# Attention weights split out of the PSUM bank that holds the exponentials, in a fused attention and gated-MLP kernel

## The chip, the core and the metric

The kernel runs on one core of a Trainium2 chip. The metric is the device time of one execution in microseconds, the median over the runs shown. Five engines work side by side, each through its own queue in order: TensorE (PE; its weight loads are PEld), VectorE (DVE), ScalarE (ACT), GpSimd (POOL) and SyncE (SP, which here only issues DMAs). Matmuls write to PSUM, which has 8 banks of 512 float32 values per partition; everything else is in SBUF. POOL does not work on PSUM in this kernel: whatever it reads lies in SBUF.

## What is computed

Eight batches of 448 tokens. Attention with 12 heads of 64, with normalised q and k, and then an MLP that is gated across tokens:

```python
# attention, per batch and head; q, k, v: (8, 12, 448, 64)
q_n, k_n = rmsnorm(q, g_q), rmsnorm(k, g_k)
scores = (1 / 8) * q_n @ k_n.T
attn = exp(scores - max(scores, axis=-1))
attn = attn / (sum(attn, axis=-1) + 1e-9)
x = attn @ v                                   # heads joined: (8, 448, 768)
# MLP
h = gelu_tanh(x @ w_in)                        # 768 -> 1024
u, v = h[..., :512], h[..., 512:]
v_n = (v - mean(v)) / sqrt(var(v) + 1e-6) * g_ln
v_s = einsum('ts,bsd->btd', w_sg, v_n) + b_sg[None, :, None]
out = x + (u * v_s) @ w_out                    # 512 -> 768
```

## The kernel before

Matmuls run on 16-bit operands. To keep float32 accuracy most operands are split into a high part (float16 of the value) and a low part (float16 of what the high part leaves), and the products that matter are summed in PSUM.

**Attention.** Heads are done in pairs, 48 pairs in all, 6 to a batch. A pair has 896 rows of scores, cut into 7 tiles of 128 rows by 448 columns; tile 3 holds the tails of both heads. In `scores(i)` a tile goes through these steps:

- L411: two matmuls on PE (four for tile 3) write the scores into a PSUM bank `s`; there are `NS` = 4 such banks.
- L414: DVE takes the negated row maximum `nm`.
- L416: ACT takes the exponential, writes it to an SBUF tile `a` (`NA` = 4 buffers) and the row sums to a small SBUF tile `sums`. After this the bank `s` is free.
- L420 and L422: once per group of tiles (`RG`: tiles 0-1, 2-3, 4-6) DVE makes the scaled reciprocals `rc` of the row sums.
- L430 or L432: the high part `a * rc` as float16, by POOL for the tiles in `PT` (0, 3, 6; in the first batch `PT0`, 0, 2, 4, 6) and by ACT for the others.
- L433: the low part `a * rc - high` on DVE, after the high part.
- L436: SP issues a DMA that transposes the two parts of two tiles (one for the last) into `at`, which `pv` multiplies with v (L453, L455) one pair later.

POOL also does most of the splitting of q and k: L344, L345 and L348, for 47 pairs (the first is split on DVE). ACT also issues the loads of q and k (L269).

**MLP.** `moe(b)` runs one batch behind the attention, in steps that are woven into it. Its matmuls use `NM` = 3 PSUM banks: `mv_` (x times the v half of `w_in`, four tiles of tokens), `mu_` (the u half, four tiles of features), `ms_` (the mix across tokens), `mo_` (the output). Gelus run in clusters, since each cluster loads the gelu table and then the exp table. Tiles that must wait for their cluster stay in their bank, or are copied to SBUF first: `mv_` tile 3 (L523) and `mu_` tiles 0 and 1 (L580). For the first and the last batch (`early`) the `mv_` matmuls start while that batch's last heads are still to come: three token tiles advance together, block by block, and the short tile 3 follows.

**Order.** The code yields pieces of scores, pv, weights and MLP in fixed proportions, and a list scheduler then sets the order on each engine from priorities and buffers. So a change of the buffers or of the engine of one step moves the work around it too.

Of the kernel before, what the change touches and what calls it, by code (L numbers as in the profile page):

```python
# [8 lines left out]
F32 = mybir.dt.float32  # L9
# [14 lines left out]
# places in the order of the work that the MLP and its gelus are moved by  # L24
MOFF, MOFF0, GP = 200, 100, 350
# steps of the weights and of the MLP per pair of heads (first, second, middle, last batch)
WR, M0, M1, MR, ML = 3, 8, 7, 11, 11
# pairs of heads at which the first MLP begins and by which the weights are done
I0, WD = 5, 6
# tiles of the scores that share a reciprocal; that are transposed together; whose high part GpSimd  # L30
# makes (in the first batch)
RG = ((0, 2), (2, 4), (4, 7))
TG = (2, 2, 2, 1)
PT, PT0 = (0, 3, 6), (0, 2, 4, 6)
# buffers
NS, NV, NM = 4, 1, 3
NQK, NVR, GV, RAWB = 2, 2, 3, 3
NA, NAH, NAT, NQT, NVH, HLB = 4, 4, 2, 2, 2, 2
# [6 lines left out]
def kernel(  # L45
# [64 lines left out]
    def newton(y, x, t):  # L110
        """y, a guess of x ** -0.5 within 3.5%, made better by a step of third and one of second order."""
# [8 lines left out]
    def pow2_scale(name, part, pool):  # L120
        """part [rows, n] holds sums of squares. Gives the power of two that takes
        every element of the tensor below 2^14 * 1.04, and its inverse."""
# [16 lines left out]
    W = {}  # L139

    def decode(dst, raw, tmp):
        """float64 words (low, high) to float32; magnitudes below float32's normal range give 0."""
# [10 lines left out]
    def weights():  # L153
        nonlocal mlp
        ctx_w = ExitStack()
        # w_in's parts take the place of its float32 values, one K block after the other
# [46 lines left out]
        # w_sg with its rows and columns in the order of the tokens on chip, and the  # L203
        # last 64 columns twice, so that both halves of the partitions get them
# [51 lines left out]
    # A head's tokens on chip: 128 c + p is token 3 p + c for c < 3 (blocks m0, m1, m2), 384 + p the  # L256
    # tail t. A pair of heads A, B is 7 columns of 128 rows: A's m0, m1, m2, then the tails of A and B
    # in one, then B's m0, m1, m2; so A's keys are in the order (m0, m1, m2, t), B's in (t, m0, m1, m2).
# [32 lines left out]
    def load_v(i):  # L291
        """A head's v in 7 columns: m0, m1, m2, (t, m0a), (m0b, m1a), (m1b, m2a), (m2b, t), with a and b
        the halves of a block: what meets the blocks of A's transposed weights and, from (t, m0a) on, of B's."""
# [17 lines left out]
    def v8(x):  # L311
        """Of a pair's columns A's 0..3 and B's 3..6."""
        return bass.AP(tensor=x.tensor, offset=x.offset, ap=[list(x.ap[0]), [10 * D, 2], [1, 4 * D]])
# [43 lines left out]
    def vsquares(i):  # L357
        """The sums of squares of the GV pairs of heads from i on."""
# [30 lines left out]
    def parts_of(t):  # L389
        """Tile t of a pair's 896 rows of scores: (rows of the tile, head)."""  # L390
        if t == CM:
            return [(0, HP, 0), (HP, P, 1)]
        return [(0, P, t // CK)]

    def scores(i):
# [4 lines left out]
        r["at"] = at  # L400
        for t0, t1 in RG:
            sums = sml.tile([P, 4], F32, name="sums")
            rc = sml.tile([P, 4], F32, name="rc")
            tl = []
            for t in range(t0, t1):
                ps = ps_s.tile([P, S], F32, name="s")
# [8 lines left out]
                a = att.tile([P, S], F32, name="a", bufs=NA)  # L415
                A.activation(out=a, in_=ps, func=AF.Exp, bias=nm, accum_out=sums[:, t - t0:t - t0 + 1])  # L416
                tl.append((t, a))
# [5 lines left out]
            for t, a in tl:  # L423
# [5 lines left out]
                if t in (PT if i >= NP else PT0):  # L429
# [55 lines left out]
    def moe(b, early=False):  # L485
# [20 lines left out]
        for st, (t, g) in enumerate(steps):  # L506
# [18 lines left out]
            if early and t == CM - 1 and g == NP - 1:  # L525
                cluster([gelu_v(i) for i in range(CM)], done)
# [269 lines left out]
```

## Time and profile before

| | |
|---|---|
| median of 3 runs (lowest to highest) | 1049.12 us (1044.31 to 1051.55) |
| span of the profiled execution | 1047.2 us, 17092 instructions |
| busy: PE / PEld / DVE / ACT / POOL | 809.6 / 447.3 / 899.9 / 705.4 / 504.6 us |
| the same as a share of the span | 77% / 43% / 86% / 67% / 48% |
| high parts made by ACT / by POOL | 186 / 150 |
| DMA | 177.74 MB, mean 170 GB/s |

Busy time is what an engine's instructions took; waiting and issuing DMAs are not in it. A row of groups reads: line, engine, operation, output tile <- input tiles, shapes, x count | busy us, mean ns of one | idle time of the engine just before them and what ended it. A bank or buffer that is late shows up as idle time of the instruction that needs it, ended by the one that freed it. Matmul records overlap each other, so a high busy share of PE does not by itself make it the limit.

### The profile page before, as it was taken

What the parts mean: (1) busy time and instruction counts of PE and PEld (TensorE: products, weight loads), DVE (VectorE), ACT (ScalarE), POOL (GpSimd) and SP (SyncE); (2) the same over time, 40 slices, a digit from 0 to 9 for tenths busy, and PEclk for the clock granted to TensorE, in tenths of its full rate; (3) what the DMA queues carried; (4) which work ended last, traced back from release to release, by engine and by line L of the source; (5) the groups of instructions that cost most, each with busy time, mean ns of one, the idle gap of its engine ahead of it and who ended that gap; (6) DMA issues with size and microseconds to landing.
All of it is one profiled execution on the core that took longest, in us unless ns stands there. A gap on an engine that the chain in (4) does not pass through costs nothing. (4 is left out here: it accounts for less than half of the span.)

```text
span 1047.2 us, 17092 instructions
## 1 busy us (share of the span) xinstructions
PE 809.6 (77%) x5652; PEld 447.3 (43%) x5652; DVE 899.9 (86%) x1959; ACT 705.4 (67%) x1418; POOL 504.6 (48%) x435
## 2 busy tenths in 40 slices
PE   0333556757689798888979899887979799799998
PEld 0111222424454346444644357343634365346546
DVE  4999979999789997999979998999889988999430
ACT  2565787676677777677767767587667686877441
POOL 1777745637536463443545372545455443535021
PEclk9666688888899899899999899999989999999999
DMA  5969589685989979996797879994989779838501
GB/s 144 254 174 244 125 179 215 160 185 108 207 180 206 194 156 206 173 217 152 162 213 181 167 149 196 202 211 106 207 190 195 148 166 201 180 89 174 110 1 61
DMA packets 528217, 177.74 MB, mean 170 GB/s; under 512 B 472257, under 2 KB 521985, under 8 KB 528129
## 3 DMA queue, kind: packets, MB, share of 16 engines
q1 hardware_dynamic: 484928, 144.07, 66.6%
q10 hardware_dynamic: 43200, 32.59, 11.3%
q8 instruction: 44, 0.72, 0.3%
q14 instruction: 45, 0.36, 0.1%
HBM read 54.58 MB, written 11.01 MB: 63 GB/s over the span
## 5 line engine op out<-in xcount | busy, mean ns | idle before, releaser
L433 DVE SCALAR_TENSOR_TENSOR ahl<-a,rc,ahl 128x448 f16<-128x448 f32 x336 | 289.6, 886 | 32.1 <-POOL ahl L430 22.0
L416 ACT ACTIVATE a<-s,nm 128x448 f32<-128x448 f32 x336 | 211.0, 630 | 124.7 <-DVE ahl L433 78.0
L411 PE MATMUL s<-qt 128*128 128x448 f16 (+1 forms) x768 | 192.2, 388 | 120.8 <-ACT a L416 63.5
L430 POOL TENSOR_SCALAR ahl<-a,rc 128x448 f16<-128x448 f32 x150 | 117.3, 786 | 230.0 <-DVE rc L422 99.9
L414 DVE TENSOR_REDUCE nm<-s 128x1 f32<-128x448 f32 x336 | 200.2, 610 | 18.5 <-PE s L411 18.0
L432 ACT ACTIVATE ahl<-a,rc 128x448 f16<-128x448 f32 x186 | 118.1, 662 | 61.5 <-DVE rc L422 34.2
L411 PEld LDWEIGHTS <-qt 128*128 128x128 f16 (+1 forms) x768 | 57.2, 105 | 209.2 <-issue 127.8
L345 POOL TENSOR_TENSOR qk<-qk,ny 128x896 f32<-128x896 f32 x47 | 83.2, 1792 | 70.6 <-DVE ny L118 34.4
L348 POOL TENSOR_TENSOR hl<-qk,hl 128x896 f16<-128x896 f32 x47 | 95.7, 2037 | 34.4 <-ACT hl L347 26.3
L453 PE MATMUL pv<-at,vl 128*64 128x384 f16 x384 | 68.2, 368 | 56.7 <-DMA at<-ahl 44.8
L344 POOL TENSOR_TENSOR qk<-qk,gg 128x448 f32<-128x448 f32 x47 | 58.9, 1255 | 77.0 <-ACT sqk L324 76.8
L453 PE MATMUL pv<-at,vh 128*64 128x384 f16 x672 | 91.0, 357 | 0.0
L575 PEld LDWEIGHTS <-wi 128*128 128x128 f16 x576 | 57.4, 102 | 61.8 <-issue 15.9
L455 PE MATMUL pv<-at,vh 128*64 128x64 f16 x672 | 78.7, 202 | 0.0
L611 POOL TENSOR_TENSOR gt<-gt,u 128x448 f32<-128x448 f32 x32 | 39.0, 1221 | 79.0 <-DVE gt L610 59.2
L453 PEld LDWEIGHTS <-vl 128*64 128x64 f16 x384 | 30.7, 118 | 90.0 <-DMA at<-ahl 37.0
L416 ACT ACTIVATION_READ_ACCUMULATOR a<-s,nm 128x1 f32 x336 | 65.9, 196 | 0.0
L325 DVE TENSOR_REDUCE ss<-sqk 128x14 f32<-128x896 f32 x48 | 51.5, 1073 | 15.5 <-ACT sqk L324 15.2
L347 ACT ACTIVATE hl<-qk 128x896 f16<-128x896 f32 x48 | 45.3, 945 | 25.6 <-DMA qk<-in_k_dram 11.4
L324 ACT ACTIVATE sqk<-qk 128x896 f32<-128x896 f32 x48 | 45.3, 944 | 21.7 <-DVE ss L325 11.2
L453 PEld LDWEIGHTS <-vh 128*64 128x64 f16 x672 | 50.2, 120 | 18.6 <-issue 0.8
L420 DVE TENSOR_SCALAR rc<-sums 128x2 f32<-128x2 f32 x144 | 52.1, 364 | 7.1 <-ACT a L416 6.5
(995 smaller groups left out, 2096.0 us busy)
## 6 DMA issues: line engine op xcount, KB each, us to landing
qk<-in_k_dram ACTq DMA_DIRECT2D x48, 192.0 KB, 3.6
vr<-in_v_dram SPq DMA_DIRECT2D x16, 576.0 KB, 4.9
vr<-in_v_dram SPq DMA_DIRECT2D x32, 288.0 KB, 5.9
out_dram<-ot ACTq DMA_DIRECT2D x24, 384.0 KB, 3.8
qk<-in_q_dram ACTq DMA_DIRECT2D x46, 192.0 KB, 3.6
raw<-in_moe_w_in_dram SPq DMA_DIRECT2D x12, 512.0 KB, 4.9
vr<-in_v_dram SPq DMA_DIRECT2D x32, 96.0 KB, 4.9
at<-ahl SPq DMA_TRANSPOSE x192, 3.8
```

The costliest lines, as they stand in the source:

```text
L344: E.tensor_tensor(out=qk[:, C7:], in0=qk[:, C7:], in1=gg.unsqueeze(1).broadcast_to([P, C7, D]), op=ALU.mult)
L345: E.tensor_tensor(out=qk, in0=qk, in1=r["rs"].unsqueeze(2).broadcast_to([P, SSW, D]), op=ALU.mult)
L348: E.tensor_tensor(out=hl[:, 0:SSW, 1], in0=qk, in1=hl[:, 0:SSW, 0], op=ALU.subtract)
L411: mm(out=ps[p0:p1], lhsT=qt[:, t * P + p0:t * P + p1], rhs=qt[:, k0:k0 + S], start=(n == 0), stop=(n == 1))
L414: V.tensor_reduce(out=nm, in_=ps, axis=AX.X, op=ALU.max, negate=True)
L416: A.activation(out=a, in_=ps, func=AF.Exp, bias=nm, accum_out=sums[:, t - t0:t - t0 + 1])
L430: G.tensor_scalar(out=hl[:, 0], in0=a, scalar1=sc, scalar2=1.0, op0=ALU.mult, op1=ALU.mult)
L432: A.activation(out=hl[:, 0], in_=a, func=AF.Copy, scale=sc)
L433: V.scalar_tensor_tensor(out=hl[:, 1], in0=a, scalar=sc, in1=hl[:, 0], op0=ALU.mult, op1=ALU.subtract)
L453: mm(out=o[:, 0:SM].rearrange("p (c n) -> p c n", c=CM), lhsT=w, rhs=at[:, h * CK:h * CK + CM, blk], start=(n == 0), stop=(n == n_s - 1), ...
L455: mm(out=o[:, SM:S], lhsT=w, rhs=at[:, CM, blk, h * HP:(h + 1) * HP], start=False, stop=(n == n_s - 1), skip_group_check=True)
L575: done = mm(out=ps[:, 0:S], lhsT=ww[:, g, f * P:(f + 1) * P], rhs=xx, start=(n == 0), stop=(n == 17))
```

## The change

It does four things.

1. The exponential (L419 now) overwrites the scores in their own bank: `a` and its four buffers are gone. The row sums of a group go to columns 448 to 451 of the bank of the group's first tile.
2. The high part is made from that bank by ACT for every tile; POOL has none left. DVE makes the low part (L433 as before) from the bank too. The bank is free only after that.
3. There are 5 score banks in place of 4, and 2 MLP banks in place of 3 (one bank for pv as before, 8 in all).
4. The MLP copies `mv_` tiles 3 and 0 to SBUF before the gelus (before: 3 alone; `VC`), and in the first and last batch only two token tiles advance block by block; the others follow one by one.

```diff
-PT, PT0 = (0, 3, 6), (0, 2, 4, 6)
+VC, UC = (3, 0), (0, 1)
-NS, NV, NM = 4, 1, 3
+NS, NV, NM = 5, 1, 2
-NA, NAH, NAT, NQT, NVH, HLB = 4, 4, 2, 2, 2, 2
+NAH, NAT, NQT, NVH, HLB = 4, 2, 2, 2, 2
...
         for t0, t1 in RG:
-            sums = sml.tile([P, 4], F32, name="sums")
...
-                ps = ps_s.tile([P, S], F32, name="s")
+                bank = ps_s.tile([P, 512], F32, name="s")
+                ps = bank[:, 0:S]
+                if t == t0:
+                    sums = bank[:, S:S + 4]
...
-                a = att.tile([P, S], F32, name="a", bufs=NA)
-                A.activation(out=a, in_=ps, func=AF.Exp, bias=nm, accum_out=sums[:, t - t0:t - t0 + 1])
-                tl.append((t, a))
+                A.activation(out=ps, in_=ps, func=AF.Exp, bias=nm, accum_out=sums[:, t - t0:t - t0 + 1])
+                tl.append((t, ps))
...
-                if t in (PT if i >= NP else PT0):
-                    G.tensor_scalar(out=hl[:, 0], in0=a, scalar1=sc, scalar2=1.0, op0=ALU.mult, op1=ALU.mult)
-                else:
-                    A.activation(out=hl[:, 0], in_=a, func=AF.Copy, scale=sc)
-                V.scalar_tensor_tensor(out=hl[:, 1], in0=a, scalar=sc, in1=hl[:, 0],
+                A.activation(out=hl[:, 0], in_=ps, func=AF.Copy, scale=sc)
+                V.scalar_tensor_tensor(out=hl[:, 1], in0=ps, scalar=sc, in1=hl[:, 0],
                                        op0=ALU.mult, op1=ALU.subtract)
...
-        steps = [(t, g) for t in (CM, *range(CM)) for g in range(NP)]
+        order = (CM, *range(CM))
+        steps = [(t, g) for t in order for g in range(NP)]
         if early:
-            steps.sort(key=lambda x: (x[1], x[0]))
-            steps = [x for x in steps if x[0] < CM] + [x for x in steps if x[0] == CM]
+            steps = ([(t, g) for g in range(NP) for t in range(2)]
+                     + [(t, g) for t in order for g in range(NP) if t == CM or t > 1])
...
-            if t == CM and g == NP - 1 and not early:
-                A.activation(out=vg[:, tiles[t][1]], in_=ps[:, 0:FH], func=AF.Copy)
+            if t in VC and g == NP - 1 and not early:
+                A.activation(out=vg[:, tiles[t][1]], in_=ps[:, 0:DH if t < CM else FH], func=AF.Copy)
...
-            if early and t == CM - 1 and g == NP - 1:
-                cluster([gelu_v(i) for i in range(CM)], done)
+            if early and t == 1 and g == NP - 1:
+                cluster([gelu_v(i) for i in range(2)], done)
```

The scheduler moves a good deal around this. The next listings show three places; the names in brackets are what an instruction waits for (an engine, or a DMA queue, with the semaphore's number).

On PE, score matmuls of a pair in the middle of the kernel. Before, when a bank comes free:

```order
L411 LDWEIGHTS qt
L411 MATMUL s<-qt 128x448 [waits Activation_49]
L411 LDWEIGHTS qt
L411 MATMUL s<-qt 128x448
L411 LDWEIGHTS qt
L411 MATMUL s<-qt 128x448 [waits Activation_49]
L411 LDWEIGHTS qt
L411 MATMUL s<-qt 128x448
L411 LDWEIGHTS qt
L411 MATMUL s<-qt 64x448 [waits Activation_49]
L411 LDWEIGHTS qt
L411 MATMUL s<-qt 64x448
```

And now, in a batch's pair behind the `mu_` matmuls:

```order
L415 LDWEIGHTS qt [waits DMAHW5_49]
L415 MATMUL s<-qt 128x448 [waits DVE_49]
L415 LDWEIGHTS qt
L415 MATMUL s<-qt 128x448
L415 LDWEIGHTS qt [waits DVE_49]
L415 MATMUL s<-qt 128x448 [waits PE_49]
L415 LDWEIGHTS qt
L415 MATMUL s<-qt 128x448
L415 LDWEIGHTS qt
L415 MATMUL s<-qt 128x448 [waits DVE_49]
L415 LDWEIGHTS qt
L415 MATMUL s<-qt 64x448 [waits DVE_49]
```

The bank was released by ACT (the exponential); it is now released by DVE (the low part), and tiles come in longer rows, up to the five banks.

On ACT, exponentials (`s,nm`) and high parts (`rc`) of a middle pair. Before:

```order
L432 ACTIVATE ahl<-a,rc 128x448 [waits DVE_49,Activation_49]
L432 ACTIVATE ahl<-a,rc 128x448 [waits Activation_49]
L324 ACTIVATE sqk<-qk 128x896 [waits DMAHW6_49,DMAHW5_49,DMAHW7_49,DMAHW4_49,DMAHW0_49]
L416 ACTIVATE a,sums<-s,nm 128x448 [waits DVE_49] x2
L416 ACTIVATE a,sums<-s,nm 128x448 [waits DVE_49,PE_49]
L580 ACTIVATE u<-mu__6488 128x448 [waits PE_49]
```

And now:

```order
L419 ACTIVATE s<-s,nm 128x448 [waits Activation_49]
L419 ACTIVATE s<-s,nm 128x448 [waits DVE_49]
L419 ACTIVATE s<-s,nm 128x448 [waits PE_49,Activation_49]
L269 DMA qk<-in_k_dram 128x2x192 [waits DMAHW1_49]
L613 ACTIVATE gh<-gt 128x448 [waits Pool_49]
L432 ACTIVATE ahl<-s,rc 128x448 [waits DVE_49,Activation_49]
L432 ACTIVATE ahl<-s,rc 128x448
L432 ACTIVATE ahl<-s,rc 128x448 [waits DVE_49,Activation_49]
L432 ACTIVATE ahl<-s,rc 128x448
```

High parts of two or more tiles now stand in a row on ACT. Many exponentials wait for ACT itself, since the row sums of one tile go to the bank of another.

On DVE, low parts of a middle pair. Before:

```order
L386 SCALAR_TENSOR_TENSOR vl<-vr,v_s,vh 128x512 [waits DMAHW6_49,Activation_49]
L433 SCALAR_TENSOR_TENSOR ahl<-a,rc,ahl 128x448 [waits DMAHW3_49,Pool_49]
L433 SCALAR_TENSOR_TENSOR ahl<-a,rc,ahl 128x448 [waits DMAHW2_49,Activation_49]
L113 TENSOR_TENSOR nt<-nt,ny 128x28 [waits DVE_49]
L113 TENSOR_TENSOR lt<-lt,ly 128x4 [waits DVE_49]
L433 SCALAR_TENSOR_TENSOR ahl<-a,rc,ahl 128x448 [waits Activation_49]
L414 TENSOR_REDUCE nm<-s 128x1 [waits PE_49]
```

And now:

```order
L423 TENSOR_SCALAR rc<-s 128x3 [waits Activation_49]
L425 RECIPROCAL rc<-rc 128x3 [waits DVE_49]
L423 TENSOR_SCALAR rc<-s 128x2 [waits Activation_49]
L425 RECIPROCAL rc<-rc 128x2 [waits DVE_49]
L433 SCALAR_TENSOR_TENSOR ahl<-s,rc,ahl 128x448 [waits DMAHW1_49,Activation_49]
L433 SCALAR_TENSOR_TENSOR ahl<-s,rc,ahl 128x448 [waits Activation_49]
L433 SCALAR_TENSOR_TENSOR ahl<-s,rc,ahl 128x448 [waits DMAHW5_49,Activation_49]
L418 TENSOR_REDUCE nm<-s 128x1 [waits PE_49] x2
```

A low part waited for POOL or ACT; all now wait for ACT. The transposes that SP issues stay at 192.

More of the change, by code (lines that the diff above doesn't have):

```diff
@@ L422, in scores @@
             V.reciprocal(out=rc[:, 0:n], in_=rc[:, 0:n])
-            for t, a in tl:
+            for t, ps in tl:
                 if t in starts:
@@ L521, in moe @@
                                   rhs=ww[:, g, DH + e * FH:DH + (e + 1) * FH], start=first, stop=final)
-            if t == CM and g == NP - 1 and not early:
-                A.activation(out=vg[:, tiles[t][1]], in_=ps[:, 0:FH], func=AF.Copy)
+            if t in VC and g == NP - 1 and not early:
+                A.activation(out=vg[:, tiles[t][1]], in_=ps[:, 0:DH if t < CM else FH], func=AF.Copy)
                 psv[t] = vg[:, tiles[t][1]]
-            if early and t == CM - 1 and g == NP - 1:
-                cluster([gelu_v(i) for i in range(CM)], done)
+            if early and t == 1 and g == NP - 1:
+                cluster([gelu_v(i) for i in range(2)], done)
             if st % 2 == 1:
                 yield
-        cluster([gelu_v(t) for t in ((CM,) if early else (CM, *range(CM)))], done)
+        cluster([gelu_v(t) for t in order if not early or t == CM or t > 1], done)
         for t in range(CK):
@@ L578, in moe @@
                         yield
-            if f < 2:
+            if f in UC:
                 A.activation(out=u[f], in_=ps[:, 0:S], func=AF.Copy)
```

## The prediction

> **What bounds the kernel now.** I read the busy time by stage first (the table of windows), then the costliest groups of the long middle stage, then the spread of single durations, and last what each engine waited for. The stages are the first 300 us (weights and the first batch), 300 to 950 us, and the tail, where only the last MLP is left. The columns are the stretch, its length, and busy us (with the count of instructions) of PE, PEld, DVE, ACT and POOL, then the clock, DMA share and GB/s.
>
> ```profile
> core 0: us, PE busy (x) PEld busy (x) DVE busy (x) ACT busy (x) POOL busy (x), PEclk, DMA share, GB/s
> 0.00:300.00 300.00, 157.04 (x960) 78.36 (x962) 266.24 (x553) 191.33 (x384) 169.91 (x139) 0.78 0.79 182
> 300.00:950.00 650.00, 564.09 (x4079) 312.47 (x4077) 595.65 (x1320) 469.38 (x948) 315.44 (x272) 0.95 0.84 178
> 950.00:1047.20 97.20, 88.48 (x623) 56.42 (x619) 37.98 (x88) 44.72 (x88) 19.28 (x25) 0.99 0.34 79
> ```
>
> In the middle DVE is busy 595.65 of 650 us (91.6%), ACT 72%. PE shows 87%, but its records overlap and DVE hardly ever waits for it: the row of the row maximum (L414) below has 5.3 us of idle time ended by PE in 650. So the middle is bound by DVE, and the tail by PE (88.48 of 97.20). The groups of the middle stage that the change touches:
>
> ```profile
> L433 DVE SCALAR_TENSOR_TENSOR ahl<-a,rc,ahl 128x448 f16<-128x448 f32 x237 | 210.7, 914 | 26.4 <-POOL ahl L430 18.0 <-ACT ahl L432 8.4
> L416 ACT ACTIVATE a<-s,nm 128x448 f32<-128x448 f32 x237 | 148.8, 630 | 84.3 <-DVE ahl L433 47.5 <-DVE nm L414 23.7 <-DVE rc L420 3.6
> L414 DVE TENSOR_REDUCE nm<-s 128x1 f32<-128x448 f32 x237 | 140.5, 610 | 5.5 <-PE s L411 5.3
> L432 ACT ACTIVATE ahl<-a,rc 128x448 f16<-128x448 f32 x136 | 85.9, 662 | 38.2 <-DVE rc L422 18.0 <-issue 8.2 <-DVE nt L116 2.6
> L430 POOL TENSOR_SCALAR ahl<-a,rc 128x448 f16<-128x448 f32 x101 | 74.1, 738 | 157.2 <-DVE rc L422 61.6 <-DVE rc L420 15.4 <-DMA at<-ahl 12.5
> L420 DVE TENSOR_SCALAR rc<-sums 128x2 f32<-128x2 f32 x68 | 21.3, 317 | 1.3 <-ACT a L416 1.1
> L420 DVE TENSOR_SCALAR rc<-sums 128x3 f32<-128x3 f32 x34 | 13.4, 393 | 5.4 <-ACT a L416 5.2
> ```
>
> The low part (L433) is DVE's largest item, 914 ns in the mean. Its median is another number. The next rows give min/median/max of single instructions, and the timeline (start, us) one of the long ones beside what POOL does then:
>
> ```profile
> L433 DVE SCALAR_TENSOR_TENSOR ahl<-a,rc,ahl x336: 658/676/2397, 40.9 to 977.9; 128x448 f16<-128x448 f32 x168
> L420 DVE TENSOR_SCALAR rc<-sums x144: 128/159/1698, 34.3 to 975.5; 128x2 f32<-128x2 f32 x96, 128x3 f32<-128x3 f32 x48
> L414 DVE TENSOR_REDUCE nm<-s x336: 584/610/626, 28.8 to 973.5; 128x1 f32<-128x448 f32 x168
> L462 DVE SCALAR_TENSOR_TENSOR xl<-pv,xh x48: 585/611/625, 75.8 to 987.8; 128x448 f16<-128x448 f32 x48
> L610 DVE SCALAR_TENSOR_TENSOR gt<-ms__5332,gw,bb x1: 685/685/685, 495.8 to 495.8; 128x448 f32<-128x448 f32 x1
> L610 DVE SCALAR_TENSOR_TENSOR gt<-ms__6887,gw,bb x1: 655/655/655, 613.4 to 613.4; 128x448 f32<-128x448 f32 x1
> 649.38 2.40 DVE L433 SCALAR_TENSOR_TENSOR ahl<-a,rc,ahl 128x448 f16<-128x448 f32 x1
> 649.40 1.89 POOL L348 TENSOR_TENSOR hl<-qk,hl 128x896 f16<-128x896 f32 x1
> ```
>
> Half of the low parts take 676 ns or less, the longest 2397, and that one lies around a whole POOL instruction of 1.89 us, which starts with it. Both read SBUF. DVE instructions that read a PSUM tensor (L414, L462) never stretch: 626 and 625 ns at most, and the two extremes of L610, which has the very form that the new low part gets (a PSUM tensor, a column of scalars, an SBUF tensor), are 655 and 685. Reading the scores from PSUM therefore takes the low part out of that collision.
>
> **The change, part by part.** Low part on DVE: 0.672 us, near the middle of L610's two ends, for 0.914 in the middle stage, so 210.7 x 0.672/0.914 = 155, a gain of 56 us. The ends are 0.611 (L462, no column of scalars) and today's 0.914.
>
> [...]
>
> Row sums on DVE (L420): the sums are read from PSUM too, and I take L420's median, 0.159 us, for all: 68 x (0.317 - 0.159) + 34 x (0.393 - 0.159) = 19 us gained; the lower end is nothing. DVE in the middle: 595.7 - 56 - 19 = 521. What other DVE instructions gain because POOL drops 74.1 us I leave at nothing.
>
> ACT takes the 101 high parts that POOL made in this stage, and reads PSUM for all of them. For a scaled ACT instruction of this size from PSUM and from SBUF, and for how far neighbours overlap:
>
> ```profile
> L584 ACT ACTIVATE u<-mu__9708,hs x1: 634/634/634, 819.4 to 819.4; 128x448 f32<-128x448 f32 x1
> L584 ACT ACTIVATE u<-mu__9633,hs x1: 617/617/617, 821.0 to 821.0; 128x448 f32<-128x448 f32 x1
> L584 ACT ACTIVATE u<-u,hs x16: 653/657/658, 221.3 to 1009.4; 128x448 f32<-128x448 f32 x16
> 823.88 0.62 ACT L416 ACTIVATE a<-s,nm 128x448 f32<-128x448 f32 x1
> 824.40 0.20 ACT L416 ACTIVATION_READ_ACCUMULATOR a<-s,nm 128x1 f32 x1
> 824.49 0.54 ACT L461 ACTIVATE xh<-pv 128x448 f16<-128x448 f32 x1
> ```
>
> From PSUM it is (0.634 + 0.617)/2 = 0.626 us, and an instruction starts 0.1 before its neighbour's end, so 101 x 0.526 = +53; the 136 that ACT made already drop from 0.662 to 0.626, -5. The exponential now writes PSUM, which no row shows ACT do; the nearest difference is that between reading the two memories (657 - 626 = 31 ns), so between -7 and +7 us for 237 of them, and I take 0. The row sums land in the bank of the group's first tile, so an exponential must wait for ACT's own write before it: in the order such waits stand at some 180 of the 336 exponentials, for some 45 now. Each costs the overlap of 0.1 us and at most as much again; 0.15 x 135 x 237/336 = +14, less 3 for high parts that lose such a wait. One more copy of a v tile per batch in that stage (about 0.6 each): +3. ACT: 469.4 + 53 - 5 + 14 - 3 + 3 = 531. So ACT passes DVE and becomes the fullest engine.
>
> Banks for scores. Today a bank is free after the exponential and `a` (4 buffers) carries the tile on; after the change the bank is held until the low part is done, and there are 5. How many tiles are in flight now? Up to a time, the score matmuls started (16 a pair for 7 tiles, so 16/7 a tile) less the low parts; the columns are as above. First the score matmuls (L411; PE and PEld), then the low parts (L433; DVE):
>
> ```profile
> 0.00:390.00 390.00, 72.24 (x274) 22.23 (x275) 0.82 0.83 183
> 0.00:510.00 510.00, 96.94 (x371) 29.21 (x372) 0.84 0.82 181
> 0.00:750.00 750.00, 146.31 (x577) 44.05 (x578) 0.87 0.83 181
> 0.00:870.00 870.00, 171.00 (x674) 50.85 (x674) 0.88 0.84 181
> ```
>
> ```profile
> 0.00:390.00 390.00, 95.15 (x113) 0.82 0.83 183
> 0.00:510.00 510.00, 134.73 (x157) 0.84 0.82 181
> 0.00:750.00 750.00, 217.29 (x246) 0.87 0.83 181
> 0.00:870.00 870.00, 256.30 (x291) 0.88 0.84 181
> ```
>
> That gives 6.9, 5.3, 6.4 and 3.9 tiles, 5.6 in the mean. A tile comes every 650/237 = 2.74 us, so it stays 5.6 x 2.74 = 15.3 us from matmul to low part. Five banks never hold more than 5. The shortest stay, for two tiles that share a reciprocal, is, from the rows above and a matmul of 0.22 us (below), two matmuls (0.44), two maxima (1.2), the second exponential with its sum (0.75), rc (0.16), two high parts (1.15) and a low part (0.67): 4.4 us without the hops between engines, so five banks could feed far more than is needed; the 15.3 is mostly queueing, 47.5 us of it the exponential's wait for an `a` buffer and 18.0 the wait for POOL's high part, both of which go. What is late next is the score matmul, waiting for DVE's low part instead of for ACT, with the MLP's matmuls queued behind it on PE.
>
> Two MLP banks in place of three: PE's waits for an MLP bank are small now (the largest of the middle, 4.5 us in all, is below), so I put the loss there at nothing, covered by PE's idle time (650 - 564 = 86 us), and at +15 us at worst. The last MLP has one of its four v tiles later: 18 matmuls at 3.34/15 = 0.22 us, +4 us on the tail, which PE sets.
>
> ```profile
> PE ms__9820 L605 <- ACT u L584: 4.5, 1, 4.5
> 881.89 3.34 PE mv__10744 L517 x15
> ```
>
> The first 300 us, from the same groups of that stage:
>
> ```profile
> L433 DVE SCALAR_TENSOR_TENSOR ahl<-a,rc,ahl 128x448 f16<-128x448 f32 x81 | 65.7, 833 | 2.6 <-POOL ahl L430 1.8 <-ACT ahl L432 0.8
> L430 POOL TENSOR_SCALAR ahl<-a,rc 128x448 f16<-128x448 f32 x41 | 37.4, 916 | 55.3 <-DVE rc L422 20.8 <-ACT a L416 19.4 <-issue 9.5
> L420 DVE TENSOR_SCALAR rc<-sums 128x2 f32<-128x2 f32 x24 | 10.8, 449 | 0.0
> L420 DVE TENSOR_SCALAR rc<-sums 128x3 f32<-128x3 f32 x11 | 5.6, 508 | 0.1
> ```
>
> DVE gains 65.7 x (1 - 0.672/0.833) = 13 and 24 x 0.290 + 11 x 0.349 = 11 us: 266 - 24 = 242, at the same fill (88.7%) 273 us; ACT gets 41 x 0.526 = 22 more, 213, and doesn't bind. Fewer tiles can be in flight, so I take half of the gain: 287.
>
> The sum. The fullest engine of the middle, ACT with 531 us, would need 580 us at DVE's present fill of 91.6%. I take 88%, 603 us, since ACT and DVE (521) now stand within 2% of each other and hand each tile to and fro with less room between. 287 + 603 + 101 = 991 us, 56 below the profiled span of 1047.2. The median of the runs shown is 1.9 above that span, so I forecast 993 us.
>
> **Rivals.** (1) The fill is kept and the exponential gets cheaper: 531 - 7 = 524, at 91.6% 572, with 273 and 97: 942 + 2 = 944 us. For it: the waits of the exponential on `a` and of the low part on POOL are gone. Against: two full engines.
>
> (2) The low part costs more from PSUM than L610 says: once more what the column of scalars adds (0.672 - 0.611 = 0.061 us). Then 237 x 0.061 = 14 us come back on DVE, which has 535 and passes ACT, 535/0.88 = 608, and the first stage loses 81 x 0.061/2 = 2.5: 1000 us with the 2. L610 speaks against it. [...]
>
> (3) The ring of banks eats the gain: a tile stays 13.5 us, so the middle takes 237 x 13.5/5 = 640, with 297 and 101: 1040 us.
>
> (4) The low part is held up by POOL as before, because one operand still lies in SBUF. DVE gains the 19 us alone, 577/0.9 = 641 us, 1041 in all with the other stages of (3). Against it: L462 and L610 have one SBUF operand too.
>
> (5) Slower: five banks are too few. The deciding point is a stay of 5 x 2.74 = 13.7 us. If the stay remained at 15.3, a tile would come every 3.06 us, the middle would take 725 us and the whole 300 + 725 + 101 + 2 = 1128; in between at 14.3 us it is 678 and about 1081. For it: tiles in flight are above 5 at three of the four times. Against it: the waits that make the stay long are those that go.
>
> **How the numbers follow.** About 1%, 10 us, is what a measurement of this kernel can tell from no change. Chances: my forecast 0.42 (own range 965 to 1035), (1) 0.20, (2) 0.06, (3) 0.12, (4) 0.04, (5) 0.16. Faster: 0.42 + 0.20 + 0.06 = 0.68; within 1%: 0.16; slower: 0.16. The range goes down to rival (1)'s 944, below which I leave 0.08, and up to 1070, which leaves about 0.1 of rival (5) out.
>
> **What would show it.** Right: the low part near 0.67 us with a maximum below 0.7; rc near 0.16; ACT the fullest engine of the middle, near 88%; POOL emptier by its high parts (74 and 37 us in the first two stages). In the waits, the score matmul behind the low part appears, but DVE and ACT have little idle time that ends on PE. Rival (1) would show ACT above 91%; (2) low parts of 0.74; (3) and (5) idle DVE and ACT with the row maximum waiting for the score matmul, and a stay (tiles in flight times period) above 13 us; (4) low parts of 2 us. My sum is wrong above all if the 88% is.

## The result and the profile after

The changed kernel takes 1059.01 us (median of 10 runs), the kernel before 1047.31 (median of 10, on the same chip). The ratio is 1.0106, with a 95% interval of 1.0076 to 1.0135: slower by 1%, where 993 us had been forecast. One of the ten runs of the changed kernel took 2587.05 us, and the ratio leaves it out. The profiled execution has a span of 1063.3 us, against 1047.2.

First the busy time by stage of the changed kernel, with the columns of the prediction's first table:

```profile
0.00:300.00 300.00, 157.51 (x922) 73.62 (x922) 239.36 (x539) 198.91 (x410) 126.78 (x98) 0.75 0.79 176
300.00:950.00 650.00, 562.93 (x4067) 311.67 (x4066) 529.46 (x1324) 506.51 (x1061) 226.00 (x173) 0.94 0.82 178
950.00:1063.30 113.30, 93.75 (x666) 59.09 (x664) 41.74 (x98) 51.90 (x106) 11.47 (x14) 0.94 0.37 80
```

The work left VectorE as planned: in the middle DVE is busy 529 us instead of 596. But no engine is full there any more: DVE 81%, ACT 78%. How many tiles went through meanwhile? The row maximum runs once for each tile. Its windows in the kernel before (L414; DVE busy and count), and then in the changed kernel (L418):

```profile
0.00:300.00 300.00, 51.75 (x86) 0.78 0.79 182
300.00:950.00 650.00, 139.96 (x237) 0.95 0.84 178
```

```profile
0.00:300.00 300.00, 47.57 (x80) 0.75 0.79 176
300.00:950.00 650.00, 139.93 (x237) 0.94 0.82 178
```

This is the central reading: 237 tiles in 650 us in both kernels, 2.74 us each. VectorE does the same tiles in 66 us less, and all of it has become idle time. The 16 us between the two spans come from the first stage, where six tiles fewer get through (6 x 2.74 = 16).

The groups of the changed kernel's page, with what ended the idle time before them:

```profile
L419 ACT ACTIVATE s<-s,nm 128x448 f32<-128x448 f32 x336 | 205.0, 618 | 95.6 <-DVE nm L418 88.2
L415 PE MATMUL s<-qt 128*128 128x448 f16 (+1 forms) x768 | 193.3, 396 | 100.1 <-DVE ahl L433 61.0
L433 DVE SCALAR_TENSOR_TENSOR ahl<-s,rc,ahl 128x448 f16<-128x448 f32 x336 | 216.6, 675 | 49.0 <-ACT ahl L432 48.0
L418 DVE TENSOR_REDUCE nm<-s 128x1 f32<-128x448 f32 x336 | 198.8, 614 | 43.4 <-PE s L415 42.2
L432 ACT ACTIVATE ahl<-s,rc 128x448 f16<-128x448 f32 x336 | 191.8, 653 | 31.3 <-DVE rc L425 13.2
```

The low part takes 675 ns in the mean. The waits go round in a circle: the score matmul waits for the low part that frees its bank (61.0 us), the row maximum for the score matmul (42.2), the exponential for the row maximum (88.2), the low part for the high part (48.0). In the kernel before, the wait of the row maximum for the score matmul was 18 us over the whole span:

```profile
DVE nm L414 <- PE s L411: 18.0, 14, 5.3
```

### The profile page after: what moved, and what is told of

It is laid out like the page before. It is cut to its first block, busy times and chain, and to the rows that moved or that the text cites. A ratio compares the mean times of both kernels' runs of the same rounds, so it can differ in the third digit from the quotient of the medians.

```text
span 1063.3 us, 16981 instructions
## 1 busy us (share of the span) xinstructions
PE 814.2 (77%) x5652; PEld 444.4 (42%) x5652; DVE 810.5 (76%) x1959; ACT 757.3 (71%) x1574; POOL 364.3 (34%) x285
## 3 DMA queue, kind: packets, MB, share of 16 engines
q10 hardware_dynamic: 43200, 32.59, 10.7%
## 5 line engine op out<-in xcount | busy, mean ns | idle before, releaser
L419 ACT ACTIVATE s<-s,nm 128x448 f32<-128x448 f32 x336 | 205.0, 618 | 95.6 <-DVE nm L418 88.2
L415 PE MATMUL s<-qt 128*128 128x448 f16 (+1 forms) x768 | 193.3, 396 | 100.1 <-DVE ahl L433 61.0
L433 DVE SCALAR_TENSOR_TENSOR ahl<-s,rc,ahl 128x448 f16<-128x448 f32 x336 | 216.6, 675 | 49.0 <-ACT ahl L432 48.0
L418 DVE TENSOR_REDUCE nm<-s 128x1 f32<-128x448 f32 x336 | 198.8, 614 | 43.4 <-PE s L415 42.2
L432 ACT ACTIVATE ahl<-s,rc 128x448 f16<-128x448 f32 x336 | 191.8, 653 | 31.3 <-DVE rc L425 13.2
L344 POOL TENSOR_TENSOR qk<-qk,gg 128x448 f32<-128x448 f32 x47 | 54.2, 1153 | 297.6 <-ACT sqk L324 278.4
L415 PEld LDWEIGHTS <-qt 128*128 128x128 f16 (+1 forms) x768 | 56.0, 106 | 194.0 <-issue 135.5
L348 POOL TENSOR_TENSOR hl<-qk,hl 128x896 f16<-128x896 f32 x47 | 92.2, 1963 | 66.5 <-ACT hl L347 63.2
L453 PE MATMUL pv<-at,vh 128*64 128x384 f16 x672 | 99.6, 370 | 0.0
L455 PE MATMUL pv<-at,vh 128*64 128x64 f16 x672 | 81.5, 207 | 0.0
L453 PEld LDWEIGHTS <-vh 128*64 128x64 f16 x672 | 51.0, 125 | 26.1 <-issue 6.0
L324 ACT ACTIVATE sqk<-qk 128x896 f32<-128x896 f32 x48 | 45.7, 955 | 17.9 <-DVE ss L325 11.4
L419 ACT ACTIVATION_READ_ACCUMULATOR s<-s,nm 128x1 f32 x336 | 53.0, 158 | 0.0
L518 PEld LDWEIGHTS <-xh 128*128 128x128 f16 x288 | 29.3, 107 | 55.4 <-issue 22.9
L455 PEld LDWEIGHTS <-vh 128*64 128x64 f16 x672 | 49.9, 123 | 4.4 <-issue 4.4
```

Of the source, the lines that this page charges most:

```text
L344: E.tensor_tensor(out=qk[:, C7:], in0=qk[:, C7:], in1=gg.unsqueeze(1).broadcast_to([P, C7, D]), op=ALU.mult)
L348: E.tensor_tensor(out=hl[:, 0:SSW, 1], in0=qk, in1=hl[:, 0:SSW, 0], op=ALU.subtract)
L415: mm(out=ps[p0:p1], lhsT=qt[:, t * P + p0:t * P + p1], rhs=qt[:, k0:k0 + S], start=(n == 0), stop=(n == 1))
L418: V.tensor_reduce(out=nm, in_=ps, axis=AX.X, op=ALU.max, negate=True)
L419: A.activation(out=ps, in_=ps, func=AF.Exp, bias=nm, accum_out=sums[:, t - t0:t - t0 + 1])
L432: A.activation(out=hl[:, 0], in_=ps, func=AF.Copy, scale=sc)
```

## The experiments

Three theories were stated first. R: the five score banks, held until the low part, set the pace (a ring of places). M: the two MLP banks cost the time. A: the high parts moved to ScalarE cost it. A place, here and below, is a bank or an `a` buffer that one tile takes up; a tile is in flight between its score matmul and its low part. All ratios below are to the kernel before, measured on the same chip, with the 95% interval behind them. The planner lays every kernel out anew, so that each edit also changes the order of the work around it.

**One score bank fewer.** The changed kernel with

```diff
-NS, NV, NM = 5, 1, 2
+NS, NV, NM = 4, 1, 2
```

> The changed kernel with 4 score banks in place of 5, one bank left unused, all else the same. Theory R (the five score banks, held until the low part, set the pace): a tile stays some 11.3 us in its bank, so 4 banks at the same filling give 2.71 x 5/4 = 3.4 us a tile and the time rises by more than 8%, to 1140 us or above. Theory M (the two MLP banks cost the time) and theory A (the high parts moved to ScalarE cost it): the score banks aren't what binds, so 1050 to 1085 us.

Measured: 1140.02 us, ratio 1.0889 (1.0843 to 1.0935), 81 us more than with five. The same two rows of its page as above:

```profile
L415 PE MATMUL s<-qt 128*128 128x448 f16 (+1 forms) x768 | 201.2, 409 | 130.1 <-DVE ahl L433 98.4
...
L418 DVE TENSOR_REDUCE nm<-s 128x1 f32<-128x448 f32 x336 | 200.4, 617 | 86.6 <-PE s L415 84.7
```

Both waits of the circle grew, from 61.0 to 98.4 and from 42.2 to 84.7. As R said, the ring binds with four; only R had put the time this high (1140 us or above).

**Two MLP banks alone.** The kernel before, with the change's `VC`, `UC` and order of the MLP's steps, and

```diff
-NS, NV, NM = 4, 1, 3
+NS, NV, NM = 4, 1, 2
```

> The kernel before with the change's MLP alone: 2 MLP banks, one more v tile copied, two token tiles advancing block by block in the first and last batch; the attention as before with 4 score banks, one bank unused. Theory M: most of the lost gain is here, so at least 3% slower than before, 1080 us or more. Theories R and A: within 1.5% of before, 1040 to 1063 us.

Measured: 1067.26 us, ratio 1.0175 (1.0133 to 1.0217), between the forecasts of M (1080 or more) and of R and A (1040 to 1063). Its windows:

```profile
300.00:950.00 650.00, 555.88 (x4016) 308.74 (x4012) 590.90 (x1325) 470.49 (x959) 309.04 (x266) 0.94 0.87 180
```

TensorE gets 4016 matmuls done in the middle against 4079 before, though two more row maxima ran there (239); so what is missing is not work on scores, and it is done in the tail.

**Shorter groups, and their control.** In the changed kernel, and then as a control in the kernel before:

```diff
-RG = ((0, 2), (2, 4), (4, 7))
+RG = ((0, 2), (2, 4), (4, 6), (6, 7))
```

> The changed kernel with reciprocal groups of 2, 2, 2 and 1 tiles in place of 2, 2 and 3: one more pair of small instructions on VectorE per pair of heads (48 x 0.33 = 16 us), but no bank waits for two partners. Theory R: the stay of the first tile of the group of three falls from 15 to about 11 us and the mean from 11.3 to about 10.6, so 2 to 5% faster than the changed kernel, 1005 to 1040 us. Theories M and A: within 1.5% of the changed kernel, 1045 to 1075 us.

> The kernel before with groups of 2, 2, 2 and 1 tiles. A control for the run that did this to the changed kernel and took 17 us off: if that gain came by the banks, there is none here, since the exponentials do not hold a bank: 1044 to 1057 us. If a shorter group is a gain of its own (shorter chain to the transposes), 1030 to 1042 us.

Measured: in the changed kernel 1042.06 us, ratio 0.9934 (0.9904 to 0.9964), that is 17 us better than the change as it was, and the only kernel here that beats the one before and does all of its work. It lies between the forecasts, just above R's 1005 to 1040. In the kernel before 1061.28 us, ratio 1.0114 (1.0081 to 1.0147), slower than either forecast there. So the grouping is no gain of its own; it paid where a tile that waits for its group holds a bank. That speaks for R, but doesn't show its reason: R expected a shorter stay in the bank, and by the count of tiles in flight (explained in the next section) the mean stay is 10.9 us (4.07 tiles, one every 650/242 us) against 10.7 in the changed kernel, a difference too small for that count to tell.

**High parts on ScalarE alone.** The kernel before with

```diff
-PT, PT0 = (0, 3, 6), (0, 2, 4, 6)
+PT, PT0 = (), ()
```

> The kernel before with every high part made by ScalarE, from the SBUF tile; 4 score banks, 4 buffers for the exponentials and 3 MLP banks as before. Theory A: ScalarE with 150 more instructions holds the chain up whatever the banks, 1055 us or more. Theories R and M: ScalarE has the room (it is at 67%), and the low part waits for GpSimd no more and meets it less, so 1000 to 1045 us.

Measured: 1060.17 us, ratio 1.0117 (1.0086 to 1.0148), in the range that A expected (1055 or more). Why was not followed further, and 1.2% is no more than a new order of the work alone can cost (shown below).

**Part of the tiles in the bank.** The kernel before (four score banks, three MLP banks); tiles 0, 3 and 6 of a pair keep `a` and GpSimd's high part, the other four stay in their bank; then the same with the shorter groups.

```diff
-                a = att.tile([P, S], F32, name="a", bufs=NA)
+                a = ps
+                if t in (PT if i >= NP else PT0):
+                    a = att.tile([P, S], F32, name="a", bufs=NA)
```

> The kernel before with one edit: tiles 1, 2, 4 and 5 of a pair (those whose high part ScalarE makes already) keep their exponentials in the PSUM bank; tiles 0, 3 and 6 keep them in SBUF with GpSimd's high part. Four score banks, three MLP banks and ScalarE's work stay as they were, so two of the three suspected costs are absent. If the relief of VectorE is worth time and only the ring, the MLP banks and ScalarE's load ate it (the sum theory): three of seven tiles give the bank back after the exponential (some 4.4 us), four after some 11 us, mean some 8.2 us, and 4 banks then allow a tile each 2.05 us, below the 2.71 us of now: 990 to 1030 us. If the ring is what binds even here (the four tiles come in pairs, tile 4 and 5 hold two banks at once): 1045 to 1075 us. If VectorE's busy time is not what sets the pace at all (the pace theory): 1040 to 1055 us.

> As the run of part in bank, with the groups that share a reciprocal of 2, 2, 2 and 1 tiles instead of 2, 2 and 3. If the ring binds there too, the tiles 4 and 5 give their banks back earlier (by one tile's 2.7 us or more) and it is 10 to 20 us faster than that run. If it does not bind, no faster, or slower by up to 5 us for one more reciprocal per pair of heads.

Measured: 1075.63 us, ratio 1.0255 (1.0225 to 1.0284), and 1063.61, ratio 1.0130 (1.0091 to 1.0170) with the shorter groups. The sum theory (990 to 1030) is wrong here. The first time is at the upper end of the range for a ring that binds here too (1045 to 1075), and shorter groups help again, by 12 us where 10 to 20 were expected from the ring. The first of the two has both kinds of low part in one kernel, from SBUF and from the bank, in two rows of its page:

```profile
L435 DVE SCALAR_TENSOR_TENSOR ahl<-a,rc,ahl 128x448 f16<-128x448 f32 x150 | 137.2, 915 | 21.4 <-POOL ahl L432 21.2
...
L435 DVE SCALAR_TENSOR_TENSOR ahl<-s,rc,ahl 128x448 f16<-128x448 f32 x186 | 124.0, 675 | 9.7 <-ACT ahl L434 9.7
```

**Row sums back in SBUF.** The changed kernel with

```diff
-                if t == t0:
-                    sums = bank[:, S:S + 4]
+            sums = sml.tile([P, 4], F32, name="sums")
```

> The changed kernel with the row sums in an SBUF tile, as before, instead of in the first tile's bank. The page of the changed kernel shows VectorE's add reading them there at some 0.16 us less each, and the two read-outs of the accumulator a little shorter. If the sums' place costs nothing (ring, MLP banks and ScalarE are the causes): 1055 to 1070 us, a few us slower for VectorE's longer adds. If waits of ScalarE on its own sums in the bank were a cause: 1035 to 1050 us.

Measured: 1063.98 us, ratio 1.0151 (1.0116 to 1.0187), no better than the change as it was (1.0076 to 1.0135), and in the range for that case. The place of the sums is not the cause.

**VectorE's load alone.** The kernel before; the row maximum takes half of the columns.

```diff
-                V.tensor_reduce(out=nm, in_=ps, axis=AX.X, op=ALU.max, negate=True)
+                V.tensor_reduce(out=nm, in_=ps[:, 0:S // 2], axis=AX.X, op=ALU.max, negate=True)
```

> The kernel before, with the row maximum taken over 224 of the 448 columns (the other half is left out). It takes from VectorE alone, some 336 x 0.27 = 90 us of busy time as the changed kernel did, with four banks, three MLP banks and ScalarE untouched. If VectorE sets the pace of the kernel before (the premise of the prediction: 92% full in the middle): 980 to 1010 us. If some other resource takes over at once (TensorE is 87% busy in the middle of every kernel so far), so that 90 us less of VectorE are worth little: 1025 to 1050 us. In the second case the changed kernel had hardly anything to win.

Measured: 1030.15 us, ratio 0.9819 (0.9775 to 0.9862). Its windows (the middle stage), and then the two groups of its page that matter:

```profile
300.00:950.00 650.00, 585.38 (x4242) 326.79 (x4241) 574.63 (x1356) 481.12 (x989) 328.97 (x283) 0.96 0.88 185
```

```profile
L433 DVE SCALAR_TENSOR_TENSOR ahl<-a,rc,ahl 128x448 f16<-128x448 f32 x336 | 305.5, 932 | 32.7 <-POOL ahl L430 30.1
...
L414 DVE TENSOR_REDUCE nm<-s 128x1 f32<-128x224 f32 x336 | 122.0, 377 | 12.7 <-PE s L411 12.3
```

The maximum dropped to 377 ns, the low parts beside GpSimd grew to 932; in all DVE is busy 847.5 instead of 899.9 us. So VectorE lost 52 us of its work and not 90 as expected; with places, MLP banks and ScalarE's work untouched, that brings 19 us (1.8% of 1049). The time is in the second forecast's range (1025 to 1050), that of little worth: VectorE may help to set the pace, but at about a third of what it is relieved of, and a new order of the work alone can be worth nearly as much (next run). VectorE is still 88% busy in the middle (574.63 of 650 us). What else holds the kernel there is open. The DMA engines, 84% busy in the middle of the kernel before, are at 88% in this row; no run lightened them.

**TensorE's load alone.** Both kernels without the matmuls of v's low part:

```diff
-        steps = [[(vl[:, h, c], c) for c in range(4)]
-                 + [(vh[:, h, (c + h * CM) % C7], c) for c in range(C7)] for h in range(2)]
+        steps = [[(vh[:, h, (c + h * CM) % C7], c) for c in range(C7)] for h in range(2)]
```

> The kernel before without the four matmul steps of vl in each pair's weights-times-values (the products with v's low part are left out): some 80 us less of TensorE in the stretch from 300 to 950 us, nothing else. If VectorE sets the pace of the kernel before: 1030 to 1050 us. If TensorE does: 950 to 1000 us.

> The changed kernel without the vl steps, as the run on the kernel before. If the ring of score banks sets the pace (matmuls of the scores wait for banks, and TensorE has slack): 1035 to 1062 us. If TensorE has taken over as the bound of the changed kernel: 970 to 1015 us, a larger gain than in the kernel before.

Measured: 1064.19 us, ratio 1.0138 (1.0105 to 1.0172), from the kernel before, and 1049.77, ratio 1.0009 (0.9981 to 1.0037), from the changed one, which is 9 us faster than the change as it was. The first lies outside both of its forecasts, the second within that of the ring. The first one's windows (the middle stage):

```profile
300.00:950.00 650.00, 539.94 (x3413) 286.55 (x3412) 592.05 (x1295) 456.70 (x923) 306.07 (x262) 0.91 0.81 175
```

TensorE runs 666 matmuls fewer there than before, but is only 24 us less busy (564.09 before), not 80: those left take longer in the mean (158 ns of busy time each, for 138). Since the kernel with fewer matmuls is slower and the other hardly faster, the number of matmuls sets the pace of neither. The first also sets a measure for the rest: taking work away made the kernel 1.4% slower. A lower clock is not the reason, since two of its six runs, at a mean granted clock of 0.89 and 0.90, took as long (1065.11 and 1060.62 us) as those at 0.86. So an edit's new order of the work can be worth about as much as the single effects of 1 to 2% above, and these runs cannot part the two.

**The single tile on GpSimd.** The changed kernel with groups of 2, 2, 2 and 1, and

```diff
+PT = (6,)
...
+                if t in PT:
+                    a = att.tile([P, S], F32, name="a", bufs=2)
+                    sums = sml.tile([P, 4], F32, name="sums")
...
+                if t in PT:
+                    G.tensor_scalar(out=hl[:, 0], in0=ps, scalar1=sc, scalar2=1.0, op0=ALU.mult, op1=ALU.mult)
+                else:
+                    A.activation(out=hl[:, 0], in_=ps, func=AF.Copy, scale=sc)
```

> The changed kernel with groups of 2, 2, 2 and 1, and the single tile's exponentials in SBUF with GpSimd's high part (its bank goes back after the exponential; ScalarE has 48 high parts less, VectorE 48 low parts that read SBUF). By the ring and ScalarE's load: 1015 to 1040 us against 1042 us with the grouping alone. If the reads of SBUF beside GpSimd cost more than both: 1045 to 1060 us.

Measured: 1058.11 us, ratio 1.0089 (1.0058 to 1.0119), 16 us worse than the grouping alone and in the second range. The gain by ring and ScalarE didn't come; that the reads of SBUF are the reason was not shown.

**All of the change but the bank.** From the run of two MLP banks: five score banks (first run), and then also all high parts on ScalarE (second run); the exponentials go to SBUF in both.

```diff
-NS, NV, NM = 4, 1, 2
+NS, NV, NM = 5, 1, 2
...
-PT, PT0 = (0, 3, 6), (0, 2, 4, 6)
+PT, PT0 = (), ()
```

> The kernel before with five score banks and two MLP banks, high parts split between GpSimd and ScalarE as before, exponentials in SBUF. It differs from the run of MLP two banks (1067 us, four score banks) by the fifth score bank alone. If the tiles in flight (9 instead of 8) still matter at this number: 1045 to 1060 us. If eight are enough: 1062 to 1072 us.

> The whole change (five score banks, two MLP banks, all high parts on ScalarE) except that the exponentials go to an SBUF tile, and the row sums with them. Against the changed kernel's 1059 us this gives the worth of the stay in the bank, gain on VectorE and loss of places together. If the places in flight (9 here, 5 after) are worth more than VectorE's cheaper low part: 1030 to 1055 us. If VectorE's relief is worth more than the places: 1065 to 1090 us; the single runs on the MLP banks and on the high parts add up to 1049 + 18 + 12 = 1079 us.

Measured: 1077.44 us, ratio 1.0295 (1.0273 to 1.0318), and 1061.34, ratio 1.0137 (1.0103 to 1.0171). Both miss their forecasts: the first is above either range, so that a ninth place brought nothing, and the second lies between its two. The second one's low parts:

```profile
L434 DVE SCALAR_TENSOR_TENSOR ahl<-a,rc,ahl 128x448 f16<-128x448 f32 x336 | 275.3, 846 | 11.3 <-ACT ahl L433 10.7
```

With the earlier run the change can now be walked in four steps: two MLP banks 1.0175, a fifth score bank 1.0295, high parts on ScalarE 1.0137, exponentials in the bank 1.0106. The last step is the heart of the change, and it takes DVE from 867.7 to 810.5 us. With the loss of places (nine become five) that comes with it, it is worth nothing that can be measured, since the last two intervals overlap. Nor do single effects add: the high parts cost 1.2% in the kernel before and bring 1.5% here.

**Fewer tiles in flight in the kernel before.** First three `a` buffers instead of four; then two, with the shorter groups (to be set against the control's 1.0114).

```diff
-NA, NAH, NAT, NQT, NVH, HLB = 4, 4, 2, 2, 2, 2
+NA, NAH, NAT, NQT, NVH, HLB = 3, 4, 2, 2, 2, 2
```

> The kernel before with three SBUF tiles for the exponentials instead of four: seven tiles in flight instead of eight, all else the same. If the number of tiles in flight sets the pace (ring): 1065 to 1100 us. If eight is more than is needed: 1045 to 1058 us.

> The kernel before with groups of 2, 2, 2 and 1 and two SBUF tiles for the exponentials: six tiles in flight instead of eight; to be set against the run with that grouping alone (1061 us). If the number in flight sets the pace: 1090 to 1150 us. If not: 1058 to 1070 us.

Measured: 1098.92 us, ratio 1.0499 (1.0467 to 1.0530), and 1188.96, ratio 1.1365 (1.1330 to 1.1399). The first is in the ring's range, the second above it. In the waits of the two kernels the exponential waits for the low part that frees its `a` (78.0 us in the kernel before):

```profile
ACT a L416 <- DVE ahl L433: 135.3, 114, 5.5
```

```profile
ACT a L416 <- DVE ahl L433: 185.6, 154, 5.0
```

The kernel before, too, loses 5% with one place fewer.

**More of them.** The kernel before with five `a` buffers (and 11 instead of 12 for the parts of the attention's output), and with six (and three instead of four `ahl`, the finished weights that wait for their transposition; its edit is not shown):

```diff
-NA, NAH, NAT, NQT, NVH, HLB = 4, 4, 2, 2, 2, 2
-NOT, NX = 2, 12
+NA, NAH, NAT, NQT, NVH, HLB = 5, 4, 2, 2, 2, 2
+NOT, NX = 2, 11
```

> The kernel before with five SBUF tiles for the exponentials instead of four, and 11 instead of 12 buffers for the parts of the attention's output to make room. If the stretch from the exponential to the low part binds at four (the trace of before has ScalarE's exponentials waiting for the low part 51 times in the middle): 1025 to 1043 us. If four are enough: 1045 to 1052 us.

> The kernel before with six SBUF tiles for the exponentials, and three instead of four buffers for the finished weights that wait for their transposition. If the stretch from the exponential to the low part binds: 1010 to 1040 us, unless the three buffers become the next ring, seen as waits of the high parts for the transposes' DMA; then 1045 to 1080 us. If four were enough and the three buffers suffice: 1045 to 1052 us.

Measured: 1065.53 us, ratio 1.0162 (1.0132 to 1.0191), and 1076.97, ratio 1.0271 (1.0236 to 1.0306). Both expected gains failed, although the exponential's wait for the low part fell from 78.0 us before to 34.9 with five and 17.9 with six:

```profile
ACT a L416 <- DVE ahl L433: 34.9, 34, 3.5
```

```profile
ACT a L416 <- DVE ahl L433: 17.9, 17, 3.1
```

So in the kernel before fewer than eight places cost time, and more brought none: here with another buffer given up, in the run of five score banks without. With five buffers, the middle is in fact faster (246 row maxima against 237), but the tail gets 689 matmuls; the kernel before had 623 there. The windows of the row maximum (L414), and then those of all work:

```profile
300.00:950.00 650.00, 146.10 (x246) 0.93 0.89 183
```

```profile
950.00:1080.00 130.00, 106.89 (x689) 65.75 (x686) 37.08 (x86) 45.63 (x83) 25.45 (x29) 0.97 0.18 47
```

With six, the sign named in the expectation for a next ring is there: GpSimd's high part waits 49.5 us for the transposes' DMA, 12.5 in the kernel before, and the time is in the range for that case. With five, whether the buffer that was given up, or the MLP work that fell behind, is the cause was not separated.

## Why the prediction was wrong

**Low part, 0.672 us (right).** In the changed kernel, min/median/max:

```profile
L433 DVE SCALAR_TENSOR_TENSOR ahl<-s,rc,ahl x336: 650/675/686, 39.3 to 987.2; 128x448 f16<-128x448 f32 x168
```

No stretching is left, though POOL is busy 226 us of the middle. Rival (4), low parts of 2 us, is out, and with 915 against 675 ns in one kernel (above) the reading of the collision holds. In the run of all but the bank, GpSimd had no high part, only its share of q and k and of the MLP, and the low parts from SBUF still took 846 ns. The traces show it one by one: in the kernel before, the 169 low parts that overlap no POOL instruction took 659 to 686 ns, while of the 167 that overlap one 106 took longer than that, up to 2397; in the changed kernel the 110 that overlap one took 686 at most. The old low part has two SBUF tensors as inputs, the new one has one. Rival (2) is out too: the medians are 676 ns from SBUF and 675 from PSUM.

**VectorE's sum in the middle, 521 us:** 529 measured, for the same 237 tiles; the step on the row sums took 0.150 us in the mean, for 0.159 reckoned. **ScalarE's, 531 us:** 507. ScalarE's term was too high by 25, so it didn't pass DVE. Its high parts came out as reckoned, 136.7 us in the middle for 85.9 + 53 - 5 = 134. But the exponentials fell by 4 us, the reading of the accumulator by 9 (last section), and the 14 - 3 us put down to waits between ScalarE's own writes are not found in its busy time. By the prediction's own rule VectorE, with 529, would then be the fullest engine, which changes the forecast by no more than 2 us; the miss comes from elsewhere.

**The fill of 88% (this step failed).** The prediction divided the fullest engine's 531 us by 0.88, and said that it is wrong above all if this is. It was 81% (DVE), and the middle's 237 tiles took 650 us instead of 603, 47 of the 72 us by which the sum of 991 missed the span of 1063. The 1059 us lie within the stated range of 944 to 1070, but on the slow side of the kernel before, which the prediction gave a chance of 0.16. The step rests on the reading that the middle is bound by DVE because DVE is 92% busy, and that was too strong. The runs show two things in its place. First, even with all places kept, VectorE's relief doesn't shorten the time in proportion: 52 us off VectorE brought 19. By that rate (an estimate from the half-maximum run, whose 1.8% isn't free of the order's own effect) the 89 us that the change took off were worth 89 x 19/52 = 33 us, not 56. In that run VectorE stayed 88% busy in the middle, the share that the prediction assumed; it fell to 81% only with the rest of the change. Second, the change paid for the relief with places. Eight tiles could be between matmul and low part (four banks, four `a`), now five can, and the waits go round by the banks (61.0 us of the score matmul for the low part). One place fewer costs 81 us after and 52 us before; what the step from eight to five costs by itself was not measured.

**The deciding point of rival (5), 13.7 us (too high).** It was 5 x 2.74, as if five banks could be full all the time. Tiles in flight, taken as the prediction does, every 20 us from 310 to 930 us (32 times); the first and last rows of the changed kernel, score matmuls (L415), then low parts (L433):

```profile
0.00:310.00 310.00, 59.87 (x196) 15.97 (x196) 0.75 0.80 178
...
0.00:930.00 930.00, 180.84 (x714) 52.36 (x714) 0.88 0.82 179
```

```profile
0.00:310.00 310.00, 52.07 (x81) 0.75 0.80 178
...
0.00:930.00 930.00, 198.38 (x308) 0.88 0.82 179
```

The mean is 3.9 of 5 (the first row gives 196 x 7/16 - 81 = 4.8, the last 4.4). It is 5.7 of 8 in the kernel before, 2.9 of 4 with four banks, and 5.4 of 7 with three `a`. In these four kernels, in which places were shown to count, they are filled to 71 to 78% in the mean, not to 100%. This is no fixed ceiling: in the changed kernel without the vl steps 4.4 of five are filled. The queueing went as forecast, the stay fell from 15.6 (5.7 x 2.74) to 10.7 us (3.9 x 2.74); but with 3.9 of five banks filled a stay of 10.7 us means one tile every 2.74 us, the old pace. The prediction's sign for rivals (3) and (5), a stay above 13 us, would have called the ring harmless. Of the rivals, (3) and (5) named the mechanism, idle DVE and ACT with the row maximum waiting for the score matmul, and were put at chances of 0.12 and 0.16.

**Two MLP banks, put at nothing, and at +15 us at worst.** Alone they cost 1.75% of 1049, 18 us. The cover named, TensorE's idle time in the middle, was real but not usable: the MLP work fell behind and was done in the tail. By the measure of the lighter-matmul run this size isn't free of the order's own effect.

**First stage, 300 us now, forecast at 287.** At 300 us 80 tiles are through instead of 86, so 16 us were lost where 13 were to be gained. The prediction took half of VectorE's gain there because of the fewer places; the sign was wrong. That the places are the cause there isn't shown: in the run with the row sums in SBUF, also with five banks, 86 tiles are through at 300 us, though the whole is no faster.

What stays open: how the last 1% splits. The parts measured alone add up to -33 + 18 (MLP banks) + 12 (high parts) = -3 us, against +11 measured, which leaves some 14 for the places; but steps walked in another order gave other sizes, so this sum is no proof. Shown is that one place fewer costs 5% in the kernel before and 8% in the changed one, that more than eight brought nothing, and that the exponentials' move into the bank, places lost with it and the rest of the change in place, is worth nothing that can be measured. Not shown is what holds both kernels to one tile every 2.74 us; the DMA engines, 84 and 82% busy in the middle, were not tested. Whether a sixth score bank would let the gain through wasn't tried: all eight banks are in use.

## What to carry to other kernels

Before a buffer is merged into the one ahead of it in a chain, count the places between first writer and last reader, before and after, and compare the tiles in flight with about three quarters of the places (71 to 78% in four kernels here), not with all of them. An engine that is 92% busy in the mean is not thereby worth its whole relief (here 52 us off VectorE brought 19): a run that lightens that engine alone (here half a maximum, one line) prices the relief first. If banks must be held through several engines, shorten the time for which a tile waits for its companions; that was the one cheap gain here, 17 us, though not much more than a new order of the work can be worth.

## What was not expected of the hardware

ScalarE got faster by writing its exponentials to PSUM: 608 ns each in the median, for 634. Min/median/max of the exponential and of the accumulator's read-out, in the kernel before (to SBUF), and then in the changed kernel (in place):

```profile
L416 ACT ACTIVATE a<-s,nm x336: 612/634/670, 29.4 to 974.8; 128x448 f32<-128x448 f32 x168
L416 ACT ACTIVATION_READ_ACCUMULATOR a<-s,nm x336: 187/193/244, 30.0 to 975.3; 128x1 f32 x168
```

```profile
L419 ACT ACTIVATE s<-s,nm x336: 581/608/740, 28.3 to 984.2; 128x448 f32<-128x448 f32 x168
L419 ACT ACTIVATION_READ_ACCUMULATOR s<-s,nm x336: 119/148/285, 28.8 to 984.7; 128x1 f32 x168
```

The medians fall by 26 and 45 ns. The two have different reasons: in the run with the row sums back in SBUF the exponential into PSUM keeps its 608 ns, but the read-out takes 203, so the shorter read-out comes with the sums' place in the bank.
